# Block 0's x loaded in half rows, W_in in two parts behind the taps' maximum, block 1's diagonal products in four slots

## The chip, the cores and the metric

The kernel runs on one core of one Trainium2 chip. The metric is the device time of one execution in microseconds (us). Before the change it is 684.11 us, the median of 8 runs (684.06 to 685.4).

## What is computed

A causal depthwise convolution over the sequence, followed by a feed-forward layer with exact gelu. The taps are a softmax over 7 weights for each of 8 heads of 24 channels.

```python
# x: (8, 4096, 192) f32, weight: (8, 7)
w = softmax(weight, axis=-1)
x_unf = x_pad[:, idx, :].reshape(B, S, K, H, group)      # 6 zeros ahead of each sequence
x1 = np.einsum('hk,bskhg->bshg', w, x_unf).reshape(B * S, 192)
h = x1 @ w_in                                            # (32768, 192) @ (192, 2048)
g = 0.5 * h * (1.0 + erf(h / sqrt(2)))
out = g @ w_out                                          # (32768, 2048) @ (2048, 192)
```

## The kernel before

**Tiling.** The 32768 tokens are cut in two halves, and a block n takes the same stretch of tokens from both: six blocks of 256 tokens and then blocks of 512 (`WS`). The 192 channels are three groups of 64, every third channel (`NP = 3`); with the two halves of the tokens they fill the 128 partitions. x lands in `xin` in four quarters q of 32 partitions (half of the tokens, half of the channels: 96 of them, `DQ`), VectorE (DVE) transposes it to channels by tokens (`trans`, L523, tile `xT`), the convolution makes `xc` in bf16, TensorE (PE) multiplies by W_in (`mm1`, L766) into the two buffers `hp`, ScalarE (ACT) applies gelu (L683) into `gT`, and PE multiplies by W_out (`mm2`, `mm2_t`, L797 and L830) into `ob`. One step u of `mm1` with its gelu is called a slice here; block 0 has 8 slices. A slice waits for the gelu two slices back, since `hp` has two buffers.

**Convolution.** From block 2 on DVE does it with scalar multiply-adds (L549, L556). For blocks 0 and 1 (`PC`) PE does it: seven products with diagonal matrices of the taps (`dg`) for each of four pieces kd (channel groups 0, 1 and the two halves of group 2), summed in PSUM (`pconv`, L716). Their inputs are bf16 copies `xTb` of `xT`, made by ACT and DVE for block 0 (L632, L580) and by GpSimd (POOL) for block 1 (L214); the results are copied to `xc` by `conv_out` (ACT L192, DVE L194). Block 0 and block 1 share the four PSUM banks of `ob` for it.

**Order.** Every engine's order is written out by hand, and semaphores tie them. On PE: 12 warm-up matmuls on zeros (L697), the products of block 0, then the 8 slices of block 0; the products of block 1 stand behind the slices that `behind` names. After each slice of block n from 1 on come parts of block n - 1's second multiplication.

**W_in.** W_in is needed whole, all 192 rows and 2048 columns in bf16, on partitions 0 to 63 and again on 64 to 127, since the two halves of the tokens are multiplied there. POOL's DMA queue loads columns 0 to 1023 to the first 64 partitions and 1024 to 2047 to the others, and DVE copies each to the other side in quarters of 256 columns (`dup(s)`, L503). The columns 0 to 256 and so on below are counted within these 1024. Slices 0 to 3 of block 0 need what was loaded; slices 4 to 7 need quarters 0 to 3 of the copies. The load has three parts, each of two transfers (`win_in`, L385) with a semaphore of its own: columns 0 to 256, 256 to 512 and 512 to 1024 (`FP`). The first part is POOL's first work; then it makes the identity for `dg` with two selects (L394), then issues the other two parts, then sets and fills the halo of block 0.

**Start of the other queues.** SP issues the taps' weights (`wsb`), two quarters of block 0's x, waits until W_in's first part has landed (`sp.wait_ge(S_WIN[0], 32)`, L880), and issues block 1's x, the four loads of W_out (L884), and the x of blocks 2 and 3. ACT issues the other two quarters of block 0's x. DVE meanwhile makes the taps: their maximum (L468, the first count of `S_PRO`), the softmax's sum and reciprocal, and `dg` (L492); only then does it transpose block 0's x. Its order after that: `conv_out` of block 0's two pieces, `dup(0)`, `dup(1)`, `dup(2)`, the transposes of block 1, `dup(3)`, `conv_out` of block 1.

**Block 0's tokens.** In block 0 a partition holds 8 tokens that follow one another, in the other blocks every 32nd. Block 0's x is loaded as one run for each partition, from the first token's half row to the last one's, 1440 floats, of which the half rows of the other 96 channels between them are not used.

Of the kernel before, what the change touches and what calls it, by code (L numbers as in the profile page):

```python
# [11 lines left out]
def bass_lightweight_conv__then__act_gelu_exact_kernel(  # L12
# [7 lines left out]
    B, SEQ, D = x.shape  # L20
# [8 lines left out]
    TB = 512  # L29
# [12 lines left out]
    NP = D // 64  # L42
# [15 lines left out]
    DQ = D // 2  # L58
# [32 lines left out]
    for n in range(NB):  # L91
        k = 64 if n == 0 or M0 <= n < M1 else 16 * NG[n] if n < NB - 1 else 32 * NG[n]
# [10 lines left out]
    def sem(name):  # L103
        return es.enter_context(nc.semaphore(name))

    def ap(t, off, pat):
        return bass.AP(t, off, pat)

    with es:
# [23 lines left out]
        ob = pst("ob", [128, 2048])  # L133

        S_WSB = sem("S_WSB")
        S_WIN = [sem("S_WIN%d" % i) for i in range(3)]
        S_WOUT = [sem("S_WOUT%d" % i) for i in range(4)]
        S_WOG = sem("S_WOG")
        S_XIN = [sem("S_XIN%d" % i) for i in range(NX)]
# [4 lines left out]
        S_PRO = sem("S_PRO")  # L144
# [51 lines left out]
        def wait_pc(e, n, p):  # L196

            if n == 0:
                e.wait_ge(S_PCA, (1, 2, 4)[p])
                if p >= 1:  # L200
                    e.wait_ge(S_PCE, p)
            else:
                e.wait_ge(S_PCE, 2 + (1, 3, 6)[p])

        NCV = NP * KS
        FQ = F // 8
        FH = F // 2
        FP = [0, FQ, 2 * FQ, FH]

        WG = [0, 4, 2, 6]  # L210

        def cast(e, n, p):
            e.wait_ge(S_TR, NP * n + p + 1)
            e.tensor_copy(  # L214
                ap(xTb[PC[n]], p * XB + HX, [[NP * XB, 128], [1, WS[n]]]),
                ap(xT[n % 2], p * XW + HX, [[NP * XW, 128], [1, WS[n]]]),
            ).then_inc(S_CAST[PC[n]])

        def cvd(n):

            return sum(NCV - NP * (m in K0) for m in range(n + 1) if m not in PC)
# [95 lines left out]
        def load(e, n, qs=(0, 2, 1, 3), sm=None):  # L317
            mb = WS[n] // 32
            if n >= NX:
                e.wait_ge(S_TR, NP * (n - NX + 1))  # L320
            for q in qs:
                off = ((q // 2) * HALF + OFF[n]) * D + DQ * (q % 2)
                if n == 0:

                    dst = [[TB // 32 * DQ, 32], [1, mb * D - DQ]]
                    src = [[mb * D, 32], [1, mb * D - DQ]]
                else:
                    dst = [[TB // 32 * DQ, 32], [DQ, mb], [1, DQ]]
                    src = [[D, 32], [32 * D, mb], [1, DQ]]
                e.dma_start(  # L330
                    ap(xin[n % NX], 32 * q * (TB // 32 * DQ), dst), ap(xt, off, src)
                ).then_inc(sm or S_XIN[n % NX], 16)
# [48 lines left out]
        @block.gpsimd  # L381
        def _(g):
            def win_in(c0, c1, sm):
                for hf in range(2):
                    g.dma_start(  # L385
                        ap(win, 64 * hf * NP * F + c0, [[NP * F, 64], [F, NP], [1, c1 - c0]]),
                        ap(wint, hf * FH + c0, [[NP * F, 64], [F, NP], [1, c1 - c0]]),
                    ).then_inc(sm, 16)

            win_in(FP[0], FP[1], S_WIN[0])  # L390
            g.wait_ge(S_MSET, 1)
            for hf in range(2):
                m = idb[64 * hf : 64 * hf + 64, :]
                g.affine_select(  # L394
                    out=m,
                    in_=m,
                    compare_op=ALU.is_equal,
                    fill=0.0,
                    base=0,
                    pattern=[[-1, 64]],  # L400
                    channel_multiplier=1,
                ).then_inc(S_IDN)
            for i in range(1, 3):
                win_in(FP[i], FP[i + 1], S_WIN[i])

            def halo(n):
                if n == 0:

                    t = xTb[0]
                    g.memset(  # L410
                        ap(t, 0, [[NP * XB, 128], [XB, NP], [32, HB]]), 0.0
                    ).then_inc(S_HALO)
                    for p in range(NP):
                        g.wait_ge(S_TR, p + 1)
                        g.tensor_copy(
                            ap(t, p * XB + 1, [[NP * XB, 128], [32, HB], [1, 31]]),
                            ap(
                                xT[0],
                                p * XW + HX + WS[0] - HL,
                                [[NP * XW, 128], [32, HB], [1, 31]],  # L420
                            ),
                        ).then_inc(S_HALO)
                    return

                t, tw = (xTb[1], XB) if n in PC else (xT[n % 2], XW)
                dst = ap(t, HF, [[NP * tw, 128], [tw, NP], [1, HB]])
                if n >= 2:
                    if n - 2 in PC:
                        wait_pc(g, n - 2, NP - 1)
                    else:  # L430
                        g.wait_ge(S_CV, cvd(n - 2))
                if OFF[n] % SEQ == 0:
                    g.memset(dst, 0.0).then_inc(S_HALO)
                    return
                g.wait_ge(S_TR, NP * n)
                if n == 1:
                    src = ap(
                        xT[0],
                        HX + WS[0] - HL + 31,
                        [[NP * XW, 128], [XW, NP], [32, HB]],  # L440
                    )
                else:
                    src = ap(
                        xT[(n - 1) % 2],
                        HF + WS[n - 1],
                        [[NP * XW, 128], [XW, NP], [1, HB]],
                    )
                g.tensor_copy(dst, src).then_inc(S_HALO)  # L448

            g.wait_ge(S_IDN, 2)  # L450
            halo(0)
            halo(1)
            for p in range(NP):
                cast(g, 1, p)
            for i in range(4):
                g.wait_ge(S_WOUT[i], 16)
                o = 2 * WG[i] * C
                g.tensor_copy(wout[:, o : o + 4 * C], woutf[:, o : o + 4 * C]).then_inc(S_WOG)
            for n in range(2, NB):
                halo(n)  # L460

        @block.vector
        def _(v):
# [34 lines left out]

            def dup(s):

                v.wait_ge(S_WIN[min(s, 2)], 32)
                for hf in range(2):
                    v.tensor_copy(  # L503
                        ap(
                            win,
                            64 * (1 - hf) * NP * F + FH + FQ * s,
                            [[NP * F, 64], [F, NP], [1, FQ]],
                        ),
                        ap(win, 64 * hf * NP * F + FQ * s, [[NP * F, 64], [F, NP], [1, FQ]]),
                    ).then_inc(S_DUPE)  # L510

            def trans(n, p):
                w = WS[n]
                if p == 0:
                    if xin_at(n) > 0:
                        v.wait_ge(S_XIN[n % NX], xin_at(n))
                    if n >= 2 and n - 2 in PC:
                        wait_pc(v, n - 2, NP - 1)
                    elif n >= 2:
                        v.wait_ge(S_CV, cvd(n - 2))  # L520
                    if n >= 1:
                        v.wait_ge(S_HALO, HC[n])
                v.transpose(  # L523
                    ap(xT[n % 2], p * XW + HX, [[NP * XW, 128], [1, w]]),
                    ap(
                        xin[n % NX],
                        p,
                        [[TB // 32 * DQ, 128], [D if n == 0 else DQ, w // 32], [NP, 32]],
                    ),
                ).then_inc(S_TR)  # L530

# [51 lines left out]
            ).then_inc(S_CASTV)  # L583
            conv_out(v, 0, 1)
            conv_out(v, 0, 4)
            for s in range(3):
                dup(s)
            for p in range(NP):
                trans(1, p)
            dup(3)  # L590
            for j in range(len(PIECES)):
                conv_out(v, 1, j)
# [101 lines left out]
        def _(t):  # L694
# [32 lines left out]
            taps = range(KS - 1, -1, -1)  # L727
# [3 lines left out]
            for kd in order:  # L731
                pconv(*seq[kd].pop(0))

            behind = {
                (0, 5): [(1, kd, k) for k in taps[:4] for kd in (0, 1)],
                (0, 6): [(1, kd, k) for k in taps[4:] for kd in (0, 1)],
                (0, 7): [(1, kd, k) for k in taps for kd in (2, 3)],
            }

            def mm1(n, i):  # L740
                w, c = WS[n], NCH[n]
# [3 lines left out]
                if i == 0:  # L745
                    if n in PC:
                        wait_pc(t, n, NP - 2)
                    else:
                        t.wait_ge(S_CV, cvd(n))
                if n == 0 and i < 3:  # L750
                    t.wait_ge(S_WIN[i], 32)
                if n == 0 and i >= 4:
                    t.wait_ge(S_DUPE, 2 * (i - 4) + 2)
                for cc in range(c):
# [122 lines left out]
        def _(sp):  # L877
            sp.dma_start(wsb[:, :], ap(wt, 0, [[KS, H], [1, KS]])).then_inc(S_WSB, 16)
            load(sp, 0, (0, 1))
            sp.wait_ge(S_WIN[0], 32)  # L880
            load(sp, 1)
# [44 lines left out]
```

## Time and profile before

| What | Value |
|---|---|
| median of 8 runs | 684.11 us (684.06 to 685.4) |
| the profiled execution | 684.44 us |
| its span, first to last instruction | 682.7 us |
| PE busy | 675.5 us, 99% of the span |
| DVE, ACT, POOL busy | 560.5, 536.3, 38.3 us |
| first product of block 0 on PE | 7.03 us after the span's start |
| first slice of block 0 | 8.90 us |
| first slice of block 1, its second part | 18.69, 19.47 us |
| first slice of block 2 | 30.26 us |

How to read it: times are in us from the first instruction of the span, durations of single instructions in ns where the text says so. A line like `L766` is the kernel's source line; `out<-in` names the tiles. In brackets stands the idle time of the engine before the instruction and what ended it. PE's matmuls are pipelined, so their durations overlap: two neighbours can each take 0.27 us and start 0.05 us apart. A wait for several semaphores is put down to the one that came last. The time "to landing" of a DMA runs from the start of its issue to the end of its last packet's write.

### The profile page before, as it was taken

What the parts mean: (1) busy time and instruction counts of PE and PEld (TensorE: products, weight loads), DVE (VectorE), ACT (ScalarE), POOL (GpSimd) and SP (SyncE); (2) the same over time, 40 slices, a digit from 0 to 9 for tenths busy, and PEclk for the clock granted to TensorE, in tenths of its full rate; (3) what the DMA queues carried; (4) which work ended last, traced back from release to release, by engine and by line L of the source; (5) the groups of instructions that cost most, each with busy time, mean ns of one, the idle gap of its engine ahead of it and who ended that gap; (6) DMA issues with size and microseconds to landing.
All of it is one profiled execution on the core that took longest, in us unless ns stands there. A gap on an engine that the chain in (4) does not pass through costs nothing.

```text
span 682.7 us, 27312 instructions
## 1 busy us (share of the span) xinstructions
PE 675.5 (99%) x12572; PEld 407.1 (60%) x12572; DVE 560.5 (82%) x907; ACT 536.3 (79%) x549; POOL 38.3 (6%) x57
## 2 busy tenths in 40 slices
PE   8999999999999999999999999999999999999998
PEld 4899655555555555555555555555555555555557
DVE  5999979888889888898888898888898888988611
ACT  6799987877777877777877778777778777778772
POOL 5025100000000000000000000000000000000000
PEclk9999999999999999999999999999999999999999
DMA  9345322234442243332334322334322444320123
GB/s 222 78 107 128 84 60 65 43 84 95 96 93 48 50 95 95 94 75 49 70 94 95 94 62 47 83 94 96 94 50 48 95 94 96 73 50 22 48 49 94
DMA packets 132994, 54.79 MB, mean 80 GB/s; under 512 B 126480, under 2 KB 132752, under 8 KB 132880
## 3 DMA queue, kind: packets, MB, share of 16 engines
q1 hardware_dynamic: 130960, 51.50, 32.2%
q8 instruction: 98, 1.61, 1.0%
q0 software_dynamic: 1248, 0.79, 0.8%
q10 hardware_dynamic: 672, 0.76, 0.4%
q14 instruction: 16, 0.13, 0.1%
HBM read 28.66 MB, written 25.17 MB: 79 GB/s over the span
## 4 chain that ended last, share of the span: by engine, by line
PE 96%; ACT 2%; DMA 1%; POOL 1%; issue 1%; DVE 0%; POOLq 0%
PE hp L766 47%; PE ob L830 42%; PE ob L797 6%; ACT gT L683 2%; DMA win<-in_moe_w_in_dram 1%; POOL win L385 0%; PE ob L716 0%; ACT osb L270 0%; DVE osb L312 0%; DVE xc L194 0%; POOL idb L394 0%; DVE osb L281 0%; POOLq L394 0%; POOLq L911 0%
## 5 line engine op out<-in xcount | busy, mean ns | idle before, releaser
L683 ACT ACTIVATE gT<-hp 128x1024 bf16<-128x1024 f32 x512 | 522.8, 1023 | 130.4 <-PE hp L766 127.1
L766 PE MATMUL hp<-xc,win 64*64 64x512 bf16 (+2 forms) x6048 | 418.8, 366 | 1.9 <-DMA win<-in_moe_w_in_dram 0.6
L830 PE MATMUL ob<-gT,wout 64*64 64x512 bf16 x5376 | 366.3, 376 | 0.0
L556 DVE SCALAR_TENSOR_TENSOR acc<-xT,wcol,acc 128x512 f32<-128x512 f32 (+1 forms) x495 | 315.6, 710 | 1.1 <-ACT acc L656 1.1
L766 PEld LDWEIGHTS hp<-xc,win 64*64 64x64 bf16 (+1 forms) x6048 | 187.7, 106 | 136.6 <-ACT gT L683 2.6
L830 PEld LDWEIGHTS ob<-gT,wout 64*64 64x64 bf16 x5376 | 172.1, 118 | 123.0
L312 DVE STREAM_TRANSPOSE osb<-ob 128x512 f32<-128x512 f32 x84 | 74.5, 889 | 101.5 <-PE ob L830 101.5
L523 DVE STREAM_TRANSPOSE xT<-xin 128x512 f32<-128x512 f32 (+1 forms) x105 | 78.3, 803 | 1.4 <-DMA xin<-in_x_dram 1.4
L556 DVE SCALAR_TENSOR_TENSOR xc<-xT,wcol,acc 128x512 bf16<-128x512 f32 (+1 forms) x99 | 65.4, 720 | 0.0
L448 POOL COPY xT<-xT 128x18 f32<-128x18 f32 x30 | 27.4, 915 | 507.1 <-DVE xT L523 483.1
L797 PE MATMUL ob<-wout,gT 64*128 64x192 bf16 x1024 | 52.2, 243 | 0.3
L797 PEld LDWEIGHTS ob<-wout,gT 64*128 64x128 bf16 x1024 | 43.6, 94 | 6.2 <-PE ob L797 0.6
L549 DVE TENSOR_SCALAR acc<-xT,wcol 128x512 f32<-128x512 f32 (+1 forms) x90 | 37.6, 473 | 1.1
L283 ACT ACTIVATE osb<-ob 128x192 f32<-128x192 f32 x4 | 1.3, 331 | 9.5 <-PE ob L797 9.5
L281 DVE COPY osb<-ob 128x192 f32<-128x192 f32 x4 | 1.4, 359 | 8.4 <-PE ob L797 8.4
L697 PE MATMUL hp<-warm 128*128 128x512 bf16 x12 | 5.3, 632 | 1.3 <-DVE warm L464 1.3
L270 ACT ACTIVATE osb<-ob 128x384 f32<-128x384 f32 x12 | 5.8, 487 | 0.0
L194 DVE CAST xc<-ob 64x256 bf16<-64x256 f32 (+3 forms) x8 | 2.8, 357 | 3.0 <-PE ob L716 2.8
L656 ACT ACTIVATE acc<-xT,wcol 128x256 f32<-128x256 f32 (+1 forms) x9 | 5.2, 574 | 0.0
L716 PE MATMUL ob<-xTb,dg 64*64 64x256 bf16 (+1 forms) x112 | 3.7, 247 | 0.9 <-ACT xTb L632 0.5
L716 PEld LDWEIGHTS ob<-xTb,dg 64*64 64x64 bf16 x112 | 2.6, 106 | 2.6 <-ACT xTb L632 1.4
L697 PEld LDWEIGHTS hp<-warm 128*128 128x128 bf16 x12 | 1.6, 144 | 4.0 <-issue 2.8
(32 smaller groups left out, 23.2 us busy)
## 6 DMA issues: line engine op xcount, KB each, us to landing
out_dram<-osb SPq DMA_DIRECT2D x122, 192.0 KB, 3.1
xin<-in_x_dram SPq DMA_DIRECT2D x116, 192.0 KB, 4.1
xin<-in_x_dram SPq DMA_DIRECT2D x20, 96.0 KB, 3.7
woutf<-in_moe_w_out_dram SPq DMA_DIRECT2D x4, 384.0 KB, 6.2
win<-in_moe_w_in_dram POOLq DMA_DIRECT2D x4, 96.0 KB, 4.7
win<-in_moe_w_in_dram POOLq DMA_DIRECT2D x2, 192.0 KB, 5.3
out_dram<-osb SPq DMA_DIRECT2D x8, 48.0 KB, 1.7
out_dram<-osb ACTq DMA_DIRECT2D x4, 96.0 KB, 1.9
```

Of the source, the lines that this page charges most:

```text
L270: e.activation(out=dst, in_=src, func=AF.Copy).then_inc(S_EVA)
L312: v.transpose(ap(osb[m % 2], j, [[8 * C, 128], [C // 2, TB // 32], [NP, 32]]), bank(ring(m, j)),).then_inc(S_EV)
L448: g.tensor_copy(dst, src).then_inc(S_HALO)
L523: v.transpose(ap(xT[n % 2], p * XW + HX, [[NP * XW, 128], [1, w]]), ap(xin[n % NX], p, [[TB // 32 * DQ, 128], [D if n == 0 else DQ, w // 3 ...
L549: ins = v.tensor_scalar(a, src, wk, None, ALU.mult)
L556: ins = v.scalar_tensor_tensor(dst, src, wk, a, op0=ALU.mult, op1=ALU.add)
L683: a.activation(out=ap(gT[n % 2], i * c * 2 * w, dst), in_=ap(hp[u % 2], 0, src), func=AF.Gelu,).then_inc(S_GELU)
L697: t.matmul(hp[1][:, 0:512], warm[:, 0:128], warm[:, :])
L716: ins = t.matmul(bank(kd, slice(64 * ho, 64 * ho + 64), w), dg[r, d0 : d0 + 64], xTb[PC[n]][r, x0 : x0 + w], start=(k == KS - 1), stop=(k ...
L766: ins = t.matmul(hp[u % 2][fo : fo + fw, o : o + w], ap(win, f1, [[NP * F, 64], [2, fw]]), xc[n % 2][r, p * TB : p * TB + w], start=(p == ...
L797: ins = t.matmul(bank(bb[sub], w=C), gT[m % 2][r, c0 : c0 + 128], wout[r, CH[sub][i] * C : (CH[sub][i] + 1) * C], start=(ph == 0 and i == ...
L830: ins = t.matmul(bank(ring(m, j), slice(64 * h, 64 * h + 64), w), ap(wout, 64 * hf * NF * C + CH[h][i] * C + j, [[NF * C, 64], [NP, 64]],) ...
```

## The change

It does five things, all in the first 20 us.

- Block 0's x is loaded like that of the other blocks, in half rows: 8 runs of 96 floats for each partition in place of one run of 1440. The tile is laid out with `DQ` floats for a token, and `trans` reads it so.
- W_in comes in two parts of 512 columns instead of three (256, 256, 512). `S_WIN` has two semaphores; slices 0 and 2 of block 0 wait for them, and `dup(s)` waits for part `s // 2`.
- POOL makes the identity first and then waits for the taps' maximum (`S_PRO` at 1) before it issues any part of W_in.
- On DVE `dup(2)` moves behind the transposes of block 1, beside `dup(3)`.
- Block 1's products stand behind slices 4, 5, 6 and 7 of block 0, in groups of 16, 12, 16 and 12 matmuls, instead of behind 5, 6 and 7 in groups of 16, 12 and 28.

SP's line that waits for W_in's first part is the same; the part that it waits for is now 512 columns.

```diff
-        S_WIN = [sem("S_WIN%d" % i) for i in range(3)]
+        S_WIN = [sem("S_WIN%d" % i) for i in range(2)]
...
-        FP = [0, FQ, 2 * FQ, FH]
+        FP = [0, FH // 2, FH]
...
                 off = ((q // 2) * HALF + OFF[n]) * D + DQ * (q % 2)
+                dst = [[TB // 32 * DQ, 32], [DQ, mb], [1, DQ]]
                 if n == 0:
-                    dst = [[TB // 32 * DQ, 32], [1, mb * D - DQ]]
-                    src = [[mb * D, 32], [1, mb * D - DQ]]
+                    src = [[mb * D, 32], [D, mb], [1, DQ]]
                 else:
-                    dst = [[TB // 32 * DQ, 32], [DQ, mb], [1, DQ]]
                     src = [[D, 32], [32 * D, mb], [1, DQ]]
...
-            win_in(FP[0], FP[1], S_WIN[0])
             g.wait_ge(S_MSET, 1)
             for hf in range(2):
...
                 ).then_inc(S_IDN)
-            for i in range(1, 3):
+
+            g.wait_ge(S_PRO, 1)
+            for i in range(2):
                 win_in(FP[i], FP[i + 1], S_WIN[i])
...
-                v.wait_ge(S_WIN[min(s, 2)], 32)
+                v.wait_ge(S_WIN[s // 2], 32)
...
-                        [[TB // 32 * DQ, 128], [D if n == 0 else DQ, w // 32], [NP, 32]],
+                        [[TB // 32 * DQ, 128], [DQ, w // 32], [NP, 32]],
...
-            for s in range(3):
-                dup(s)
+            dup(0)
+            dup(1)
             for p in range(NP):
                 trans(1, p)
+            dup(2)
             dup(3)
...
             behind = {
-                (0, 5): [(1, kd, k) for k in taps[:4] for kd in (0, 1)],
-                (0, 6): [(1, kd, k) for k in taps[4:] for kd in (0, 1)],
-                (0, 7): [(1, kd, k) for k in taps for kd in (2, 3)],
+                (0, 4): [(1, kd, k) for k in taps[:4] for kd in (0, 1)],
+                (0, 5): [(1, kd, k) for k in taps[4:] for kd in (0, 1)],
+                (0, 6): [(1, kd, k) for k in taps[:4] for kd in (2, 3)],
+                (0, 7): [(1, kd, k) for k in taps[4:] for kd in (2, 3)],
             }
...
-                if n == 0 and i < 3:
-                    t.wait_ge(S_WIN[i], 32)
+                if n == 0 and i in (0, 2):
+                    t.wait_ge(S_WIN[i // 2], 32)
```

## The prediction

> **What bounds the kernel now.** I read the page's busy times first. TensorE (PE) is busy nearly all the time, so outside the start only fewer or shorter matmuls would help, and the change leaves their number and shapes alone.
>
> ```profile
> PE   675.5 (99%) x12572; PEld 407.1 (60%) x12572; DVE 560.5 (82%) x907; ACT 536.3 (79%) x549; POOL 38.3 (6%) x57
> ```
>
> Then the busy time by stage: from 30.26 us to the end PE works 649.3 of 652.7 us. What can move is the time before about 20 us: whatever the first matmul of block 1 gains, the end gains, as long as VectorE (DVE) keeps ahead. So I read the chain of waits of the first 40 us (start, length, what):
>
> ```profile
> 5.19 6.02 DMA win<-in_moe_w_in_dram
> ...
> 11.35 0.85 PE hp L766 x12
> ...
> 18.09 0.42 issue
> ...
> 18.80 0.30 DVE xc L194
> ```
>
> The chain runs through W_in's last part, which frees the third slice of block 0 at 11.35, then PE and ScalarE (ACT) by turns, then block 1's diagonal products and DVE's copies of them. The 0.42 is a pause of PE that no semaphore explains. Now PE in order of time:
>
> ```profile
> 7.03 1.69 PE L716 MATMUL ob<-xTb,dg 64*64 64x256 bf16 x56 [0.48 <-ACT xTb L632]
> 8.90 0.40 PE L766 MATMUL hp<-xc,win 64*128 64x256 bf16 x4 [0.18 <-ACT xc L192]
> ...
> 11.35 1.59 PE L766 MATMUL hp<-xc,win 64*128 64x256 bf16 x24 [0.62 <-DMA win<-in_moe_w_in_dram]
> 13.29 1.74 PE L766 MATMUL hp<-xc,win 64*128 64x256 bf16 x24 [0.36 <-ACT gT L683]
> 14.97 0.63 PE L716 MATMUL ob<-xTb,dg 64*64 64x256 bf16 x16
> ...
> 17.51 0.58 PE L716 MATMUL ob<-xTb,dg 64*64 64x128 bf16 x26
> 18.51 0.24 PE L716 MATMUL ob<-xTb,dg 64*64 64x128 bf16 x2 [0.42 <-issue]
> 18.69 0.39 PE L766 MATMUL hp<-xc,win 64*128 64x256 bf16 x4
> 19.47 0.61 PE L766 MATMUL hp<-xc,win 64*128 64x256 bf16 x8 [0.38 <-DVE xc L194]
> ```
>
> The slices of block 0 (L766) start at 8.90, about 10, 11.35, 12.10, 13.29, 14.21, 15.53 and 16.75; each of the last waits for a gelu two slices back (1.02 us each) or follows products. Block 1 gets going at 19.47, when the last copy out of PSUM is done. Next the engines that feed PE:
>
> ```profile
> 4.62 0.63 DVE L492 TENSOR_TENSOR dg<-idb,wcol 128x448 bf16<-128x448 bf16 x1
> 5.95 1.33 DVE L523 STREAM_TRANSPOSE xT<-xin 128x256 f32<-128x256 f32 x3 [0.70 <-DMA xin<-in_x_dram]
> ...
> 12.82 1.34 DVE L523 STREAM_TRANSPOSE xT<-xin 128x256 f32<-128x256 f32 x3 [0.71 <-DMA xin<-in_x_dram]
> 13.40 1.33 POOL L214 CAST xTb<-xT 128x256 bf16<-128x256 f32 x3 [5.44 <-DVE xT L523]
> ...
> 14.19 0.87 DVE L503 COPY win<-win 64x768 bf16<-64x768 bf16 x2
> ```
>
> DVE waits 0.70 us for block 0's x (to 5.95) and 0.71 for block 1's (to 12.82); those casts gate the first products of block 1. Last, from issue to landing (min/median/max): block 0's x; block 1's x (half rows, beside W_in); a later load of the same half rows, issued at 33.43 with little beside it; the last three W_in transfers, two of them 192 KB.
>
> ```profile
> DMA to landing us min/median/max: 2.7/3.5/4.3
> DMA to landing us min/median/max: 3.5/3.6/4.8
> DMA to landing us min/median/max: 2.2/2.2/2.3
> DMA to landing us min/median/max: 4.6/4.9/6.0
> ```
>
> **The change part by part.** Starts below are us from the span's start.
>
> *Block 0's x.* Four transfers of 180 KB (32 runs of 5760 B) become four of 96 KB (256 runs of 384 B); issues stay two on ACT and two on SP, at 0.4 us each in both forms. The last is issued at 1.62. By the quiet row it lands 2.2 later, at 3.8; by the worst row beside W_in 4.8 later, at 6.4. W_in is not under way yet, so I take the quiet end (up to 4.6 with four in a row). What is late next is DVE's own dg, which ends at 5.25. So the transposes move from 5.95 to 5.28. ACT's cast goes 6.56 to 5.89 and takes 0.42; PE's twelfth warm-up matmul starts at 5.92 and they are 0.43 apart, so PE is free at 6.35. The products start at about 6.4 instead of 7.03: **0.63 gained** (at the bad end 0.45 lost).
>
> Against it stands the Trainium skill, "DMA: Bandwidth & Descriptors", Specifications: transfers under 512 B are below line rate, with a read-modify-write. By that rule alone x would land no earlier and this term would be 0; the landing rows above say otherwise, so I go by them.
>
> *PE's pace.* A warm-up matmul (512 columns) takes 632 ns, the steady 512-column row 366. At 7.03 the pace is already fast; no row shows when it changed after 5.92. If the products from 6.4 to 7.03 still ran slowly, about half of 0.63 is lost: 0 to 0.3, I take 0.15 **lost**.
>
> "TensorE: Matmul & The Clock Gate", Part 1, says that the clock opens at the end of a free-running window of about 3.4 us; the moment would then not move with the products, and the loss would vary by run within those ends.
>
> *W_in.* Six issues on POOL become four (0.62 to 0.78 each). The two selects (0.55) go ahead of them, at about 1.35; then POOL waits for the taps' maximum, which ends at 2.31. Issues at about 2.4, 3.05, 3.7, 4.3; POOL is free at 5.0 for the halo's memset (5.85 before), which has to be done by 5.8, so nothing behind the new wait is late. A 192 KB transfer lands 4.6 to 6.0 after its issue: first part at 7.65 to 9.05, second at 8.9 to 10.3. Only x is queued ahead of the first part, so I take 7.65 and 8.9. Slice 0 wants the first part at 8.27 (8.90 - 0.63) and slice 2 wants the second when the first gelu ends, 10.11 - 0.63 + 1.02 = 10.5. Cost 0 (up to 0.8 at the late end), and the present wait at 11.35, where the gelu had ended at 11.14, goes: **0.2 gained**.
>
> *SP.* SP issues block 1's x only after the first part has landed: 7.65 instead of 6.68; behind it stand W_out and the x of blocks 2 and 3. The four issues take 1.36 to the last, at 9.0; that lands 2.2 (quiet) to 4.8 (now) later. W_in's second part is still running, but for a shorter time than now, so I take 3.0: block 1's x at 12.0 instead of 12.8. W_out is 1.0 later at most; its last cast ends at 18.62 and PE needs it with the second group of L797 at 20.90, hidden by 2.3 less what PE gains. Block 2's x: if later by 0.5, DVE ends that block's convolution at 29.3 instead of 28.82; PE wants it at 30.26 less the gain. Hidden up to a gain of about 1.0 then, of 1.4 if it is not late.
>
> *Copies of W_in and the four slots.* With slice 0 at 8.27 the gelus start at 9.48, 10.40, 11.41; slice 4 starts at 12.48 instead of 13.29. Products follow it: 16 (0.56), slice 5 (0.76), 12 (0.46), slice 6 (0.76), 16 half-width (0.36), slice 7 (0.76), 12 (0.25). From 12.48 that ends at 12.48 + 0.76 + 0.56 + 0.76 + 0.46 + 0.76 + 0.36 + 0.76 + 0.25 = 17.15; now the same point is 18.09. **0.94 gained in all**, x and the wait for W_in included; 0.1 of it is that slice 5 no longer waits for its gelu (14.21 against 13.29 + 0.76). The pause and the three last copies behind it stay as they are.
>
> The new dependence: the products of the first slot need block 1's casts. With x at X, the rows give the first cast done at X + 1.02 and the second at X + 1.46, the slot done at X + 1.96. PE would have it done at 13.80 by itself, so X beyond 11.84 is **lost one for one**: 0.16 at 12.0. The two quarters copied behind the transposes (0.87 each) are ready at 14.2 and 15.1; slices 6 and 7 want them at 15.0 and 16.1.
>
> Sum: 0.94 - 0.15 - 0.16 = 0.63. The profiled execution took 684.44 (span 682.7), 0.33 above the median of the runs; from the median 684.11 the same step gives **683.5**.
>
> **The rivals.** *Faster by over 0.2%* (1.37 us, about what a measurement of this kernel can tell from no change): x at 11.2, nothing lost to the pace, and PE's pause of 0.63 between the last products gone; DVE's last copies then follow 0.26 earlier: 0.94 + 0.26 = 1.20, and 1.4 with the 0.2 to 0.3 by which single runs differ: 682.7. For it: the quiet landing row; against: the pause has no releaser, so nothing in the change removes it.
>
> *Slower*: the first part of W_in lands at its late end, 9.05, and block 1's x, issued behind it, 3.6 after the last issue at 10.4: X = 14.0. PE stands behind slice 4 with the products in its queue: 14.0 - 11.84 = 2.2 lost against 0.94: 1.2 slower, 685.3. At X = 12.8 it is even, from 14.2 on over 0.2% slower; with the 4.8 row X is 15.2 and the time 686.5. For it: the second part at 5.19 did take 6.0, and the first part is now twice as large and starts 1.1 us later. Against: that one was queued behind four others and met block 1's x.
>
> *No effect*: x lands at 6.4, or the pace takes back 0.3, and X is 12.6: the gains cancel, 684.1.
>
> **How the numbers follow.** Forecast and no effect together 0.50 within 0.2%; X between 12.8 and 14.2 another 0.12, also within; slower 0.15; faster 0.23. The range goes from the faster case, 682.6, to between no effect and the slower case, 685.0; the likeliest case's own range is 682.9 to 684.2.
>
> **What would show it.** Right: transposes of block 0 at 5.3 and products at 6.4; slice 2 waiting for a gelu and not for W_in; block 1's transposes at 11.2 to 12.5; PE's second run of block 1 at about 18.8. Wrong: slice 0 waiting for W_in, PE idle after slice 4 for POOL's casts, or a DVE wait for block 2's x that reaches PE near 30.

## The result and the profile after

| | before | after |
|---|---|---|
| median of the runs | 684.14 us (683.89 to 685.40, 31 runs) | 686.40 us (685.32 to 687.51, 11 runs) |
| after / before, 95% interval | | 1.0031 [1.0023, 1.0039] |
| profiled execution, its span | 684.44 us, 682.7 us | 686.34 us, 684.6 us |

The changed kernel is slower by 2.3 us. The forecast was 683.5, and the upper end of its range 685.0. The profiled executions differ by 1.90 us, and the whole of this difference lies before 33 us: the first matmul of block 2 starts at 32.17 us, where it started at 30.26 (1.91 later), and the last matmul of all starts 1.94 later.

The busy times hardly moved, as the edits leave PE's work alone:

```profile
PE   675.3 (99%) x12572; PEld 410.0 (60%) x12572; DVE 561.1 (82%) x907; ACT 536.5 (78%) x549; POOL 37.6 (5%) x55
```

The chain of waits of the first 40 us after the change (start, length, what):

```profile
3.44 6.17 DMA win<-in_moe_w_in_dram
9.63 0.35 SPq L328
...
11.51 0.45 SPq L885
...
13.54 2.42 SPq L328
...
16.98 5.64 DMA xin<-in_x_dram
22.64 1.35 DVE xT L522 x3
...
24.90 4.82 DVE acc L555 x13
...
31.54 0.50 DVE xc L555
...
32.17 0.83 PE hp L767 x12
```

Before, the chain went from W_in's last part straight to PE (the third slice of block 0). Now it goes through SP's queue: the first part of W_in takes 6.17 us from its second issue and lands at 9.61. Only then does SP issue block 1's x (L328), W_out (L885) and block 2's x (L328 again). Block 2's x lands at 22.62, DVE's convolution of it ends at 32.03, and PE has to wait for that. SP's own wait for the first part (in total, times, longest), before and after:

```profile
SPq L330 <- DMA win<-in_moe_w_in_dram: 4.6, 1, 4.6
...
SPq L328 <- DMA win<-in_moe_w_in_dram: 7.0, 1, 7.0
```

PE in order of time, after, the same places as were shown of before:

```profile
6.26 1.69 PE L716 MATMUL ob<-xTb,dg 64*64 64x256 bf16 x56 [0.27 <-ACT xTb L632]
...
9.75 1.49 PE L767 MATMUL hp<-xc,win 64*128 64x256 bf16 x24 [1.80 <-DMA win<-in_moe_w_in_dram]
...
11.72 1.72 PE L767 MATMUL hp<-xc,win 64*128 64x256 bf16 x24 [0.48 <-ACT gT L683]
13.67 0.83 PE L767 MATMUL hp<-xc,win 64*128 64x256 bf16 x12 [0.23 <-ACT gT L683]
14.64 1.04 PE L716 MATMUL ob<-xTb,dg 64*64 64x256 bf16 x16
...
18.70 0.36 PE L716 MATMUL ob<-xTb,dg 64*64 64x128 bf16 x12
...
20.09 0.61 PE L767 MATMUL hp<-xc,win 64*128 64x256 bf16 x8 [0.70 <-DVE xc L194]
...
22.45 0.83 PE L798 MATMUL ob<-wout,gT 64*128 64x192 bf16 x16 [0.76 <-POOL wout L457]
...
32.17 0.83 PE L767 MATMUL hp<-xc,win 64*128 64x256 bf16 x12 [0.19 <-DVE xc L555]
```

The products start 0.77 us earlier (6.26, before 7.03), and at slice 0 nothing of that is left: PE waits 1.80 us there for W_in and starts at 9.75 (before 8.90). Slice 2 waits for a gelu. Slice 4 starts at 13.67, 0.38 later than before. Block 1's second run starts at 20.09, 0.62 later. At 22.45 PE has waited for POOL's cast of W_out, a wait that was not there before. Three lines of before that stand against these (the same multiplication by W_out, POOL's last cast of it, and DVE's transposes of block 2's x):

```profile
20.90 0.82 PE L797 MATMUL ob<-wout,gT 64*128 64x192 bf16 x16
...
17.79 0.83 POOL L458 CAST wout<-woutf 128x768 bf16<-128x768 f32 x1 [0.63 <-DVE xc L194]
...
19.44 1.34 DVE L523 STREAM_TRANSPOSE xT<-xin 128x256 f32<-128x256 f32 x3
```

The engines that feed PE, after:

```profile
5.18 1.35 DVE L522 STREAM_TRANSPOSE xT<-xin 128x256 f32<-128x256 f32 x3
...
13.59 1.36 DVE L522 STREAM_TRANSPOSE xT<-xin 128x256 f32<-128x256 f32 x3 [2.18 <-DMA xin<-in_x_dram]
...
21.56 0.83 POOL L457 CAST wout<-woutf 128x768 bf16<-128x768 f32 x1 [0.99 <-DMA woutf<-in_moe_w_out_dram]
22.64 1.34 DVE L522 STREAM_TRANSPOSE xT<-xin 128x256 f32<-128x256 f32 x3 [2.62 <-DMA xin<-in_x_dram]
```

Block 0's x no longer holds DVE up (its transposes start at 5.18, with no wait). Block 1's x does so for 2.18 us, up to 13.59 (before 12.82), and block 2's for 2.62 us, up to 22.64 (before 19.44). W_out's last cast starts at 21.56 (before 17.79).

From issue to landing (min/median/max), after: block 0's x; the two transfers of W_in's first part; block 1's x.

```profile
DMA to landing us min/median/max: 2.7/2.9/3.0
DMA to landing us min/median/max: 4.2/5.2/6.2
DMA to landing us min/median/max: 2.2/2.4/2.6
```

In order of time, PE is 0.62 us late at block 1's second run, 1.55 at the second group of W_out's multiplication (22.45, before 20.90) and 1.91 at block 2's first slice: steps of 0.62, 0.93 and 0.36. They are not three prices that could be had back one by one. The chain above, from W_in over SP and block 2's x to 32.17, has no piece of PE in it, so block 2 would start there even if PE had not waited before.

### The profile page after: what moved, and what is told of

It is laid out like the page before. It is cut to its first block, busy times and chain, and to the rows that moved or that the text cites. A ratio compares the mean times of both kernels' runs of the same rounds, so it can differ in the third digit from the quotient of the medians.

```text
span 684.6 us, 27310 instructions
## 1 busy us (share of the span) xinstructions
PE 675.3 (99%) x12572; PEld 410.0 (60%) x12572; DVE 561.1 (82%) x907; ACT 536.5 (78%) x549; POOL 37.6 (5%) x55
## 4 chain that ended last, share of the span: by engine, by line
PE 93%; DMA 2%; DVE 1%; ACT 1%; SPq 1%; issue 1%; POOL 0%
PE hp L767 46%; PE ob L831 42%; PE ob L798 5%; ACT gT L683 1%; DMA win<-in_moe_w_in_dram 1%; DVE acc L555 1%; DMA xin<-in_x_dram 1%; SPq L328 1%; SPq L885 0%; DVE xT L522 0%; DMA wsb<-in_weight_dram 0%; ACT osb L270 0%; DVE osb L312 0%; POOL win L383 0%; DVE acc L548 0%
## 5 line engine op out<-in xcount | busy, mean ns | idle before, releaser
L767 PEld LDWEIGHTS hp<-xc,win 64*64 64x64 bf16 (+1 forms) x6048 | 190.0, 106 | 136.4 <-issue 2.5
L502 DVE COPY win<-win 64x768 bf16<-64x768 bf16 x8 | 3.4, 420 | 1.6 <-DMA win<-in_moe_w_in_dram 1.3
```

The source lines that it names most:

```text
L767: ins = t.matmul(hp[u % 2][fo : fo + fw, o : o + w], ap(win, f1, [[NP * F, 64], [2, fw]]), xc[n % 2][r, p * TB : p * TB + w], start=(p == ...
```

## The experiments

Times are medians, ratios are to the kernel before on the same chip with the 95% interval; the kernel before had medians of 684.10, 684.12 and 684.11 us in the three sets of runs. One execution of each kernel was profiled. "First part" is the W_in transfer pair that SP waits for. It had landed at 6.67 us before and at 9.61 after. In every kernel the time at which PE starts block 2 (30.26 before, 32.17 after) is the measure of what the start lost in the profiled execution.

### Each of the three edits alone

The first set asks which edit costs the time. The change's five points are taken as three edits: the x load; W_in's parts with the moment of their issue; the copies with the four slots.

*Only half rows for block 0's x (x_only).*

```diff
+                dst = [[TB // 32 * DQ, 32], [DQ, mb], [1, DQ]]
                 if n == 0:
-                    dst = [[TB // 32 * DQ, 32], [1, mb * D - DQ]]
-                    src = [[mb * D, 32], [1, mb * D - DQ]]
+                    src = [[mb * D, 32], [D, mb], [1, DQ]]
...
-                        [[TB // 32 * DQ, 128], [D if n == 0 else DQ, w // 32], [NP, 32]],
+                        [[TB // 32 * DQ, 128], [DQ, w // 32], [NP, 32]],
```

> The kernel before with only block 0's x in half rows. Queue theory (the loss comes from SP's loads, which stand behind the first part of W_in: that part landed at 9.6 us in place of 6.7): the first part stays small and early, SP goes on at 6.0 to 6.8, so 683.4 to 684.3. Rival 'half rows' (1024 short runs slow what shares the DMA engines with them): W_in's first part lands past 7.5 and the time is 685 or more. Rival 'slots': nothing of it is in here, 683.4 to 684.3.

Measured: 684.83 us (684.63 to 685.84), 1.0014 [1.0006, 1.0023]. With W_in's first part still issued at 1.32, x lands later, not earlier. Landing times from issue and DVE's first transposes:

```profile
DMA to landing us min/median/max: 2.6/4.0/4.6
...
6.58 1.34 DVE L521 STREAM_TRANSPOSE xT<-xin 128x256 f32<-128x256 f32 x3 [1.32 <-DMA xin<-in_x_dram]
```

The first transfer lands after 2.6 us, as in the changed kernel; the last after 4.6, so that DVE starts at 6.58 instead of 5.95. W_in's packets run from 2.84 on, between those of x. In the kernel before, with W_in issued at the same time, W_in's first packet comes only at 4.51, when all but 4 of x's 128 packets have started (at 4.38 to 4.63 in the other four kernels with the long runs and this issue). Beside the long runs W_in had to wait, beside the half rows it did not. So the half rows gain only where W_in is held back. The profiled execution starts block 2 at 30.47, 0.21 late, and took 684.63, 0.19 over before's. The runs' median is 0.7 over; four of the eleven runs took 685.7 to 685.8, and what those lost is in no profile. The time is above what the queue theory expected and below what 'half rows' did, and W_in's first part lands early (6.31): this loss is not SP's.

*Only W_in in two parts behind the taps' maximum (win_only).*

```diff
-        S_WIN = [sem("S_WIN%d" % i) for i in range(3)]
+        S_WIN = [sem("S_WIN%d" % i) for i in range(2)]
...
-        FP = [0, FQ, 2 * FQ, FH]
+        FP = [0, FH // 2, FH]
...
-            win_in(FP[0], FP[1], S_WIN[0])
...
-            for i in range(1, 3):
+            g.wait_ge(S_PRO, 1)
+            for i in range(2):
                 win_in(FP[i], FP[i + 1], S_WIN[i])
...
-                v.wait_ge(S_WIN[min(s, 2)], 32)
+                v.wait_ge(S_WIN[s // 2], 32)
...
-                if n == 0 and i < 3:
-                    t.wait_ge(S_WIN[i], 32)
+                if n == 0 and i in (0, 2):
+                    t.wait_ge(S_WIN[i // 2], 32)
```

> The kernel before with only W_in in two parts issued behind the taps' maximum (x as before, products in three slots, three quarters copied ahead of block 1's transposes). Queue theory: first part lands at 9 to 10 us, SP issues block 1's x there, block 2's x is transposed near 22.5 in place of 19.4 and W_out's last cast is late: 685.5 to 687. Rivals 'half rows' and 'slots': neither is in here, so within 0.6 us of before, 683.5 to 684.7.

Measured: 686.13 us (684.02 to 686.93), 1.0024 [1.0015, 1.0033], within the interval of the whole change. The first part lands at 9.78. SP's wait for it, and block 2's x and first slice:

```profile
SPq L330 <- DMA win<-in_moe_w_in_dram: 7.7, 1, 7.7
...
22.65 1.34 DVE L523 STREAM_TRANSPOSE xT<-xin 128x256 f32<-128x256 f32 x3 [2.70 <-DMA xin<-in_x_dram]
...
32.18 0.83 PE L766 MATMUL hp<-xc,win 64*128 64x256 bf16 x12 [0.79 <-DVE xc L556]
```

Block 2's x and the first slice of block 2 are within 0.01 us of where the whole change has them (22.64 and 32.17), though PE's steps on the way differ (0.55, 0.41 and 0.96 us): block 2's x sets the start of block 2, whatever PE lost before. By itself this edit makes 2.03 of the 2.26 us. The three edits' losses, 0.73, 2.03 and 0.17, come to more than the whole change's, though by no more than the intervals allow.

*Only the order of the copies and the four slots (slots_only).*

```diff
-            for s in range(3):
-                dup(s)
+            dup(0)
+            dup(1)
             for p in range(NP):
                 trans(1, p)
+            dup(2)
             dup(3)
...
-                (0, 5): [(1, kd, k) for k in taps[:4] for kd in (0, 1)],
-                (0, 6): [(1, kd, k) for k in taps[4:] for kd in (0, 1)],
-                (0, 7): [(1, kd, k) for k in taps for kd in (2, 3)],
+                (0, 4): [(1, kd, k) for k in taps[:4] for kd in (0, 1)],
+                (0, 5): [(1, kd, k) for k in taps[4:] for kd in (0, 1)],
+                (0, 6): [(1, kd, k) for k in taps[:4] for kd in (2, 3)],
+                (0, 7): [(1, kd, k) for k in taps[4:] for kd in (2, 3)],
```

> The kernel before with only the four slots for block 1's products and the third quarter's copy behind block 1's transposes. Queue theory: SP untouched, PE waits behind slice 4 for POOL's casts (about 13.9 us) for 0.5 us and gets most of it back in the last slots: 683.7 to 684.6. Rival 'slots' (PE and DVE blocked by the new order make the loss): 685 or more.

Measured: 684.27 us (683.90 to 684.95), 1.0002 [0.9993, 1.0011]: no effect that this measurement shows. The profile has block 1's second run at 19.22 and block 2 at 30.01, each 0.25 earlier; the runs don't confirm it.

### Is it SP's wait?

*The changed kernel, with SP not waiting for W_in (sp_free).*

```diff
-            sp.wait_ge(S_WIN[0], 32)
```

> The changed kernel without SP's wait for W_in's first part: SP issues block 1's x, W_out and block 2's x at once. Queue theory: W_out's last cast and block 2's transposes are no longer late (at or ahead of 19.4 us), block 2's first slice at 30.3 or earlier: 683.0 to 684.6, and what W_in loses to the shared DMA engines shows at slice 0 alone. Rivals 'slots' and 'half rows': their part stays, 685.5 or more.

Measured: 687.14 us (686.78 to 687.88), 1.0045 [1.0033, 1.0058]. The expectation of a gain failed. Block 1's x comes at 12.68, and W_out and block 2's x (22.14) are not waited for, but they take the DMA engines while W_in is under way: its parts land at 10.35 and 13.75, and PE waits for both.

```profile
10.49 1.49 PE L767 MATMUL hp<-xc,win 64*128 64x256 bf16 x24 [1.78 <-DMA win<-in_moe_w_in_dram]
...
13.89 1.49 PE L767 MATMUL hp<-xc,win 64*128 64x256 bf16 x24 [1.91 <-DMA win<-in_moe_w_in_dram]
```

Block 1's second run is then at 22.16 and block 2 at 32.95. So the wait costs what stands behind it, and taking it away gains nothing: the median is 0.7 higher than with it, though the two intervals overlap. What is left to ask is why W_in's first part is so late: its size, or the moment at which it is issued.

### Size or moment of the first part

The pair that tells them apart: 512 columns issued at the start (two_early), and 256 columns issued behind the selects and the taps' maximum (three_late). Both are edits of the kernel before, with its x and its slots.

```diff
-        FP = [0, FQ, 2 * FQ, FH]
+        FP = [0, FH // 2, FH]
...
-            for i in range(1, 3):
+            for i in range(1, 2):
                 win_in(FP[i], FP[i + 1], S_WIN[i])
```

This is two_early; the number of semaphores and the waits of DVE and PE follow the two parts, as in win_only. What was expected of it:

> The kernel before with W_in in two parts of 512 columns, the first issued at the start as before, the second behind the selects; all else as before. Theory 'size' (512 columns must all land before SP goes on, and the slowest DMA engine needs some 3 us for them): first part lands at 8 to 9.5 us, the kernel takes 685.0 to 687. Theory 'late' (the loss comes from issuing W_in 1.3 to 2 us later): first part at about 7.3, 683.9 to 684.7.

And three_late:

```diff
-            win_in(FP[0], FP[1], S_WIN[0])
...
-            for i in range(1, 3):
+            g.wait_ge(S_PRO, 1)
+            for i in range(3):
                 win_in(FP[i], FP[i + 1], S_WIN[i])
```

> The kernel before with its three parts (256, 256, 512 columns), all issued behind the selects and the taps' maximum; all else as before. 'Size': first part lands at 6.5 to 7.4 us, SP is 0 to 0.7 late, 684.0 to 685.0 (POOL's halo copies wait for the two issues more: up to 0.5 of it). 'Late': first part at 8 or more, 685.5 or more.

Measured, two_early: 685.27 us (684.31 to 685.75), 1.0015 [1.0006, 1.0024]. Issued at the start, the 512 columns still land only at 9.18. The landing of the first part, SP's wait, and block 2's first slice:

```profile
DMA to landing us min/median/max: 5.7/6.4/7.1
...
SPq L330 <- DMA win<-in_moe_w_in_dram: 7.1, 1, 7.1
...
31.07 0.83 PE L766 MATMUL hp<-xc,win 64*128 64x256 bf16 x12 [0.20 <-DVE xc L556]
```

Measured, three_late: 684.80 us (684.74 to 685.24), 1.0008 [0.9999, 1.0017]. Issued late, the 256 columns land at 6.85, 0.18 after before's:

```profile
DMA to landing us min/median/max: 3.4/3.6/3.8
...
SPq L330 <- DMA win<-in_moe_w_in_dram: 4.8, 1, 4.8
...
12.28 1.49 PE L766 MATMUL hp<-xc,win 64*128 64x256 bf16 x24 [1.50 <-DMA win<-in_moe_w_in_dram]
```

So the size sets when SP goes on. The moment has a price of its own: the last part lands at 12.15 (11.21 before), and slice 2 waits 1.50 us for it (0.62 before). In the runs that price is at the edge of what can be told: three_late's interval just reaches 1. With 512 columns the late issue (win_only, 686.13) costs 0.9 more in the median than the early one (two_early), with overlapping intervals.

### SP going on after the first of the two transfers

If the queue behind SP's wait is what costs, SP can go on earlier without the first part being smaller. The first of its two transfers (the lower 64 partitions) gets a semaphore of its own, and SP waits for that alone; PE and DVE still wait for both.

```diff
+        S_WA = sem("S_WA")
...
-                    ).then_inc(sm, 16)
+                    ).then_inc(S_WA if sm is S_WIN[0] and hf == 0 else sm, 16)
...
-            sp.wait_ge(S_WIN[0], 32)
+            sp.wait_ge(S_WA, 16)
```

Added to two_early (two_early_half):

> The run with two parts issued early, with one difference: SP goes on when the first of the first part's two transfers has landed (a semaphore of its own), not both; slices and copies still wait for both. Theory 'queue' (the late first part costs through what stands behind SP's wait: W_out and block 2's x): SP goes on at 7.0 to 7.7, block 2's transposes at 19.5 to 20.4 and no wait of PE for DVE at block 2; 684.0 to 684.8. Rival 'data' (it costs because slices 0 and 2 need the columns themselves): 685.0 to 686.0, no better than with both.

Measured: 684.58 us (684.00 to 685.99), 1.0010 [1.0001, 1.0019]. SP waits 5.4 instead of 7.1, block 2's x is back near its place, and PE does not wait for W_out:

```profile
SPq L331 <- DMA win<-in_moe_w_in_dram: 5.4, 1, 5.4
...
20.21 1.34 DVE L526 STREAM_TRANSPOSE xT<-xin 128x256 f32<-128x256 f32 x3 [0.92 <-DMA xin<-in_x_dram]
...
30.14 0.82 PE L771 MATMUL hp<-xc,win 64*128 64x256 bf16 x12
```

Of the 1.15 us that two_early loses, 0.7 comes back in the median. The runs spread over 2 us and the two intervals overlap, so this run alone doesn't show the gain; its profile shows the waits gone. In it W_in's first part also landed sooner, at 8.35.

Added to the changed kernel (after_half):

> The changed kernel with the same difference: SP goes on when the first of the first part's two transfers has landed. 'Queue': SP at 6.9 to 8, block 2's transposes at 19.6 to 21 in place of 22.6, 684.3 to 685.6. 'Data': 686 or more.

Measured: 685.31 us (684.71 to 685.97), 1.0016 [1.0007, 1.0025]. Of 2.26 us, 1.1 comes back; the two intervals barely meet (1.0023 and 1.0025). In the profile PE waits neither for W_out nor for block 2's x. What it still waits for is W_in, whose parts land at 9.17 and 11.47:

```profile
9.30 1.49 PE L772 MATMUL hp<-xc,win 64*128 64x256 bf16 x24 [1.08 <-DMA win<-in_moe_w_in_dram]
...
11.60 1.49 PE L772 MATMUL hp<-xc,win 64*128 64x256 bf16 x24 [0.81 <-DMA win<-in_moe_w_in_dram]
...
20.86 1.35 DVE L525 STREAM_TRANSPOSE xT<-xin 128x256 f32<-128x256 f32 x3 [1.09 <-DMA xin<-in_x_dram]
```

The profiled execution (684.76, block 2 at 30.61, so 0.35 late) is among this kernel's fastest. What the slower runs lose, up to 1.2 us more, is in no profile.

### Attempts at a faster version

*The changed kernel with W_in in the three parts of before (three_parts)*: `FP = [0, FQ, 2 * FQ, FH]`, three semaphores, `for i in range(3)` behind the same wait.

> The changed kernel with W_in in three parts (256, 256, 512) instead of two, still behind the taps' maximum. 'Size': first part lands at 6 to 7 us and SP goes on there; W_out's last cast and block 2's transposes are near 19 us; 683.2 to 684.6. 'Late': as the changed kernel, 685.5 or more.

Measured: 685.51 us (684.77 to 686.91), 1.0023 [1.0014, 1.0032]. The first part lands at 6.80 and SP goes on there, as 'size' has it, but the time is the one that 'late' gave: the early first part brings back 0.9 us in the median and leaves 1.4. The last part lands at 12.21, and slice 2 waits for it. Block 1's x, issued beside it, lands later still:

```profile
12.35 1.49 PE L766 MATMUL hp<-xc,win 64*128 64x256 bf16 x24 [1.55 <-DMA win<-in_moe_w_in_dram]
...
13.90 1.34 DVE L521 STREAM_TRANSPOSE xT<-xin 128x256 f32<-128x256 f32 x3 [3.03 <-DMA xin<-in_x_dram]
```

*The same without the wait for the taps, and the halo's memset ahead of W_in (best).*

```diff
-            g.wait_ge(S_PRO, 1)
+            g.wait_ge(S_IDN, 2)
+            g.memset(
+                ap(xTb[0], 0, [[NP * XB, 128], [XB, NP], [32, HB]]), 0.0
+            ).then_inc(S_HALO)
             for i in range(3):
                 win_in(FP[i], FP[i + 1], S_WIN[i])
...
-                    g.memset(
-                        ap(t, 0, [[NP * XB, 128], [XB, NP], [32, HB]]), 0.0
-                    ).then_inc(S_HALO)
```

> The changed kernel with W_in in three parts (256, 256, 512), issued behind the selects and the memset of block 0's halo but without the wait for the taps' maximum, so that POOL is free for the halo copies at 5.8 us. 'Size': block 0's x lands by 5.3, first part at 6 to 6.7, 682.8 to 684.0. 'Late': 0.7 us earlier than the changed kernel's W_in, so about 685 to 685.8.

Measured: 684.73 us (684.17 to 686.25), 1.0011 [1.0002, 1.0020]. This is between the two expectations. W_in is issued from 2.00 on, 0.64 earlier than in the changed kernel, and block 0's x lands at 6.17 in place of 5.05, not by 5.3 as expected. The same wait is left at slice 2 (1.54 us, to 12.51), the last part landing at 12.37.

*The kernel before with the four slots, and SP going on after the first of the two transfers (slots_half)*: the edits of slots_only and of two_early_half together, W_in in three parts.

> The kernel before with the four slots, and with SP going on when the first transfer of W_in's first part (256 columns) has landed. SP starts some 0.3 us earlier than before, so block 1's x, for which DVE waits 1.6 us with the slots, W_out and block 2's x come earlier by as much, unless W_in gives it back: 'queue' 683.6 to 684.3; 'data' 684.1 to 684.8, since W_in's last part then lands later.

Measured: 684.54 us (684.05 to 685.19), 1.0005 [0.9996, 1.0014]. SP goes on at 6.51, but block 1's x comes no earlier than in slots_only (12.73, there 12.71), block 2 starts at 30.11, and the time is the one that 'data' gave. None of the versions beat the kernel before.

## Why the prediction was wrong

*Block 0's x* was right in its size: 0.63 forecast, 0.77 found, with the transposes at 5.18 (5.28 forecast) and the products at 6.26 (6.4). One term was off and cost nothing: an issue was put at 0.4 us "in both forms" and takes 0.60 to 0.70 in half rows, so that the last is at 2.01, not 1.62; the landings of 2.7 to 3.0 were short enough to hide it. The cover was named rightly, "W_in is not under way yet", and x_only shows what it is worth: beside W_in the last x transfer takes 4.6 us and the same edit makes the transposes 0.63 later. The place of the gain was right, its way to the end was not: slice 0 waits for W_in, and the 0.77 ends there.

Against the step stood the rule of the Trainium skill, "DMA: Bandwidth & Descriptors", Specifications, that transfers under 512 B are below line rate. The landings here show no loss from the 384-B runs: nearly alone (W_in's first packet comes at 4.21, x's last ends at 4.60) they land in 2.7 to 3.0 us, where the 5760-B runs with nearly twice the bytes took 2.7 to 4.3. What costs them is company: 4.0 in the median and 4.6 at most with W_in issued among them. On that the same page (Queues, rings and completion order) says that a DMA engine takes a packet of each queue in turn. The x_only trace, with W_in's packets from 2.84 on between those of x, is in line with it; it does not tell which engine moved which packet, and before's trace, where W_in's packets came only behind x's long runs, shows no such turns.

*PE's pace*: 0.15 was to be lost, nothing was. The products took 1.69 us, as before. The warm-up's mean matmul fell from 632 to 577 ns, so the pace changed within the warm-up this time:

```profile
L697 PE MATMUL hp<-warm 128*128 128x512 bf16 x12 | 4.7, 577 | 1.3 <-DVE warm L463 1.3
```

That was luck. Nothing in the change touches the warm-up, yet its last matmul takes 0.63 us in one execution and 0.38 in another (before, two_early_half):

```profile
5.92 0.63 PE L697 MATMUL hp<-warm 128*128 128x512 bf16 x1
...
5.33 0.38 PE L700 MATMUL hp<-warm 128*128 128x512 bf16 x1
```

In eight of the thirteen profiled executions the faster pace begins between 4.2 and 5.5 us, in the other five not before the last warm-up matmul. This agrees with the free-running window of "TensorE: Matmul & The Clock Gate", Part 1, by which the moment varies from run to run. The 366 ns set against the warm-up was the mean of a row of several shapes; the 0.38 us is of the same shape.

*W_in* was mis-sized. The text gave 7.65 to 9.05 for the first part, and took the early end because "Only x is queued ahead of the first part". It landed at 9.61, beyond the late end. Of the 1.96 us, 0.39 is the issue (the part's second transfer was issued at 3.44, not 3.05) and 1.6 the landing: the first transfer took 4.2 us, the second 6.2, not 4.6. The reason given left out the part's own first transfer, of 192 KB too, which is issued ahead of the second. two_early and three_late show that what counts for this landing is the size: in all runs with SP's wait, 512 columns land at 8.3 to 9.8 whether issued at the start or behind the taps, 256 columns at 6.3 to 6.9. So slice 0, forecast at 8.27, came at 9.75, and the *Copies* step's slice 4 at 13.67, where 12.48 was forecast. Slice 2 waits for a gelu and not for W_in, as forecast, but at 11.72.

The rule of the *Copies* step held: with x at 13.59 it has the first slot done at 13.59 + 1.96 = 15.55, and slice 5 starts at 15.61. From there its own rows put the last group of products at 18.65, and it starts at 18.70. So the rule was right and x was late, by 1.75 past the 11.84, and none of the 0.94 came about. "The pause" of 0.42 us that was to stay is not there after; without that, block 1's second run would have been later still.

*SP* is the step that failed. It reads "W_out is 1.0 later at most" and "Block 2's x: if later by 0.5": the first follows from the early end of W_in alone, and the second is given no working and is less than the 1.0 by which SP was to be late. The same text had 9.05 as the late end, by which SP goes on 2.4 us later; but those 2.4 us were only run through block 1's x (rival *Slower*), never through the two loads behind it, whose covers it gave as 2.3 and 1.4. SP went on 2.9 us later, and what stands behind it was moved by more: W_out's last landing 3.8 us (21.51, before 17.74), block 2's x 3.2 us (22.62, before 19.42). Both are past their covers, and block 2's x alone, 3.2 later less the cover of 1.4, accounts for 1.8 of the 1.91 us. In the runs, after_half shows what SP's queue is worth: 1.1 of the 2.26 us comes back when SP goes on earlier. two_early_half points the same way within the spread of its runs, and sp_free shows that the wait could not simply go. What is left goes with W_in itself: after_half's slices 0 and 2 still wait 1.08 and 0.81 us for it, and three_parts, with SP going on at 6.8, still loses 1.4 us, with slice 2 waiting 1.55 for W_in's last part and DVE 3.03 for block 1's x beside it. The *W_in* step had "Cost 0 (up to 0.8 at the late end)".

The rival *Slower* had the right mechanism (the first part late, SP's queue behind it, PE behind the slots), with 0.15 of the chance, and a price for only one of the three loads in that queue. The list of what would show the forecast wrong had named two of the three signs: slice 0 waiting for W_in, and DVE's wait for block 2's x reaching PE near 30. The third, PE waiting for W_out, was not on it.

What stays open: why the first part of 512 columns takes more than twice as long as one of 256. From W_in's first packet to the part's last signal it is 5.4 us after (from 4.21) and 4.7 in two_early, against 2.2 before (from 4.51), for twice the bytes. A first part of 512 columns made of smaller transfers was not tried. Open too is what the slower runs of one kernel lose: most of these kernels spread over 1 to 3 us, and one execution of each was profiled.

## What to carry to other kernels

When an edit changes when a waiting queue goes on, take the late end of what it waits for through every transfer behind the wait, and set each against its own cover; the first one behind is not always the one that decides. A load's semaphore is full only with its last signal, so what gates others should be small: here a part of twice the bytes held its waiters 2.5 us longer from the same issue (two_early), and two parts were not better than three for needing fewer issues. A load that is made fast by holding another back has only moved the time: ask at once who wants the one held back.

## What the runs showed of the hardware

- The last landing signals lagged. A pair of W_in transfers gives 32 signals, 16 for each transfer. Of the changed kernel's first part, the 24th came at 7.84, the 30th at 8.23, the 31st at 8.93 and the 32nd at 9.61; of before's first part, of half the bytes, the 24th at 6.48 and the 32nd at 6.67. So the last two signals hold SP and PE 1.4 us longer than the first thirty. Before's second part, also of 256 columns, had its 31st signal at 7.43 and its last at 8.83, so small size alone does not exclude it.
- W_in's packets took 114 ns in the mean (median 98, longest 854) in runs of 1024 B (512 columns of bf16, after), and 61 (median 60, longest 380) in runs of 512 B (before). W_in as a whole moved no faster: from the start of its first packet to that of its last 6.94 us after (4.21 to 11.15), 6.18 before (4.51 to 10.69).
- Issuing 256 runs of 384 B at the start took ACT and SP 0.60 to 0.70 us a transfer, 32 runs of 5760 B 0.33 to 0.44. Of the changed kernel's later issues of half rows on SP, up to 23 us, most took 0.35 to 0.46, but the first of block 2's x, right behind W_out's, 2.42, and two of block 3's and 4's x 1.80 and 1.00.
